# Forgetting attention with a spectral mix: one 8192 B row where two 4096 B rows of weights were loaded, with a spectrum shifted to fit

## The chip, the cores and the metric

The kernel runs on one core of one Trainium2 chip. The metric is the device time of one execution in microseconds (us). It is a single launch that reads all inputs from the chip's main memory (HBM) and writes the output there. A core has five engines that run side by side and meet through semaphores: TensorE (PE, the matmuls, with PEld for its weight loads), VectorE (DVE), ScalarE (ACT), GpSimd (POOL) and SyncE (SP). Transfers between HBM and the on-chip memory (SBUF, 128 partitions) run on 16 DMA engines; in this kernel POOL issues the loads and SP the stores. Matmuls write to PSUM, which DVE and ACT read.

## What is computed

Two steps, of which the second takes the first one's output.

```python
def _attn_ref(q, k, v, f):                      # [8, 8, 576, 64], f [8, 8, 576]
    scores = matmul(q, k.T) / sqrt(64)
    cum = cumsum(log(clip(f, 1e-4, 1.0)), axis=-1)
    scores = where(causal, -1e9, scores + cum[..., :, None] - cum[..., None, :])
    return matmul(softmax(scores), v)

def _moe_ref(x, w_r, w_i, w_ch):                # x [8, 576, 512], w_r, w_i [64, 512, 512]
    X = rfft(x, axis=1)                         # only the 64 lowest modes are mixed
    Xr, Xi = real(X[:, :64]), imag(X[:, :64])
    Yr = einsum('bmd,mde->bme', Xr, w_r) - einsum('bmd,mde->bme', Xi, w_i)
    Yi = einsum('bmd,mde->bme', Xr, w_i) + einsum('bmd,mde->bme', Xi, w_r)
    u = x + irfft(Y)                            # Y is 0 above mode 63
    return u + maximum(u @ w_ch, 0)
```

The inputs are f32. The weights w_r and w_i alone are 64 x 512 x 512 x 4 B x 2 = 134 MB, and each of their values is used once for the eight batches.

## The kernel before

**Stages.** First comes attention, in 32 pairs of heads (the loop over `i` with `scores`, `av`, `norm`, `trans`, `turn_v`, `back_v`); each pair's output goes to `x_all` as bf16, and `dft` (L546, L567) multiplies it with a basis of sines and cosines, which gives the 64 modes' spectrum. Then comes the *tail*, a loop over weight tiles that are left, and then the output: for 18 steps `base`, `rest` and the lines from L1013 to L1058 build `u` and `u @ w_ch` in PSUM, join them and store them.

**Units and chunks.** The 64 modes are taken as 16 units `u` of four modes. A unit's weights are four tiles (`u`, `dc`) of 1 MB in SBUF, `[128, 4096]` bf16, loaded from f32 with the type changed on the way. For `dc` 0 and 1 they hold rows 0 to 255 of the matrices. Tiles with `dc` 2 are w_r and with `dc` 3 w_i, rows 256 to 511, two neighbouring rows on each partition: a contiguous read of 2 x 512 x 4 = 4096 B per partition and mode, which lands as 2048 B. For `dc` below 2, units below 8 are read by single rows of 2048 B (L170) and the others as pairs of rows too (L179). `issue_w` issues the next tile of the list `wseq` on POOL; the code for `dc` 2 and 3 is L191.

**Where the tiles lie.** Most tiles come from `wpool`, seven buffers of 8 KB per partition, taken in turn; seven early tiles are `guests` in memory that is free then (`x_all`, `yx`). A load waits until PE has used the tile that had the buffer before. `wseq` begins with the 28 tiles of `early` (all of `dc` 0, and `dc` 1 of units 0 to 11), which are all multiplied between the attention's pairs, from the tenth on (`spec_early`). The tail then takes (u, 2), (u, 3) for units 0 to 11, and (u, 1), (u, 2), (u, 3) for units 12 and 13; then (15, 1), (15, 2), the three of unit 14, and (15, 3) last, in four parts of one mode. Three of the tiles are loaded in two cuts (`cuts`): 30 and 98 partitions, or 20 and 108.

**The spectrum.** For rows 256 to 511 it is `XP`, `[128, 2, 24, 64]`: partition p holds row 256 + 2p (index 0) and 257 + 2p (index 1), then 24 columns (minus imaginary, real, imaginary, for eight batches) and 64 modes. `by_pair` picks 16 columns of it that start at the real part for w_r and at minus the imaginary part for w_i. `spec_mms` (L229) multiplies a tile with it, eight matmuls of 512 columns for a tile (two rows x four modes), into the bank `A` of the unit. When the last tile of the unit is through, DVE adds what the early tiles gave (`Yb`, L906) and `to_rows` (L840 and the lines behind it) turns it into `YT`.

**What stands between the tiles.** In the tail's loop, `xw(b)` (L719 to L737, for eight units from 2 to 10) multiplies one batch of `x_all` with `w_ch` ahead of time, before the matmuls of the unit's `dc` 3. From unit 12 on, `folds` puts finished modes into `x_all` and `XW` (L743 to L796), with adds on POOL (L790). On L891 stand fillers: matmuls of 512 columns into a bank that nobody reads, four of them ahead of the fourth tile from the end of the list and eight ahead of the third; on L699 another eight ahead of the second. The very last tile is multiplied in `spec_cols` (L241), part by part.

**Order.** It is written by hand (`manual_schedule`): each engine takes its instructions in program order, and the framework adds the semaphore waits. `issue_w()` is called once behind each `spec_mms` of the tail.

Of the kernel before, what the change touches and what calls it, by code (L numbers as in the profile page):

```python
# [10 lines left out]
F32 = mybir.dt.float32  # L11
BF16 = mybir.dt.bfloat16
# [11 lines left out]
def kernel(  # L24
# [26 lines left out]
    NW = 7  # L51
    NX = 12
    NL = 8
    ML = 4 * NL
    XROW = 24 * ML + 32
    scale = 1.0 / math.sqrt(Dh)
# [5 lines left out]
    ctx.enter_context(tc.manual_schedule())  # L62

    const = ctx.enter_context(tc.tile_pool(name="const", bufs=1))
    wpool = ctx.enter_context(tc.tile_pool(name="wpool", bufs=NW))

    yx = const.tile([128, 8, 1280], F32, name="yx")
    x_all = const.tile([128, NEB, B, NSB, 128], BF16, name="x_all")
# [15 lines left out]
    wn = const.tile([128, NPAIR, 9], F32, name="wn")  # L84
    coef = const.tile([128, 1], F32, name="coef")
    accT = const.tile([128, NEB, B, 8], F32, name="accT")


    actx = ExitStack()
# [39 lines left out]
    early += [(u, 0) for u in range(NL, NU)] + [(u, 1) for u in range(NL, NX)]  # L129
    wseq = early[:]  # L130
    for u in range(NU - 2):
        wseq += ([] if (u, 1) in early else [(u, 1)]) + [(u, 2), (u, 3)]
    wseq += [(NU - 1, 1), (NU - 1, 2)] + [(NU - 2, dc) for dc in (1, 2, 3)] + [(NU - 1, 3)]
    wtile = {}
    wissued = [0]
# [8 lines left out]
        17: yx[:, 6:8, :].rearrange("p k e -> p (k e)").bitcast(BF16),  # L144
    }

    cuts = {(4, 2): (30,), (7, 2): (20,), (10, 2): (20,)}

    def by_rows(u, dc):

# [2 lines left out]
    def issue_w(half=None):  # L153
        n = wissued[0]
        if n >= len(wseq):
            return
        u, dc = wseq[n]
        if half != 1:
            if n in guests:
                t = 2 if by_rows(u, dc) else 4  # L160
                w8 = guests[n][:, 0 : 8 * D].rearrange("p (t m e) -> p t m e", t=t, e=D)
            else:
                shape = [128, 2, 4, D] if by_rows(u, dc) else [128, 4, 2, D]
                w8 = wpool.tile(shape, BF16, tag="w8", name="w8")
            wtile[(u, dc)] = w8
        w8 = wtile[(u, dc)]
        if by_rows(u, dc):
            for t, src in enumerate((moe_w_r, moe_w_i)):
                if half in (None, t):
                    nc.gpsimd.dma_start(  # L170
                        w8[:, t, :, :],
                        src[4 * u : 4 * u + 4, dc * 128 : (dc + 1) * 128, :].rearrange("m p e -> p m e"),
                    )
        elif dc < 2:
            src = (moe_w_r, moe_w_i)[dc]
            step = 4 if half is None else 2
            for j in range(2 * (half or 0), 4 if half != 0 else 2, step):
                m = 4 * u + j
                nc.gpsimd.dma_start(  # L179
                    w8[:, j : j + step, :, :].rearrange("p m r e -> p m (r e)"),  # L180
                    src[m : m + step, 0:256, :].rearrange("m (p r) e -> p m (r e)", r=2),
                )
        elif half != 1:
            src = (moe_w_r, moe_w_i)[dc - 2]
            ends = (0,) + cuts.get((u, dc), ()) + (128,)
            parts = [(0, 4, p0, p1) for p0, p1 in zip(ends, ends[1:])]
            if n + 1 == len(wseq):
                parts = [(j, 1, 0, 128) for j in range(4)]
            for j, step, p0, p1 in parts:
                m = 4 * u + j  # L190
                nc.gpsimd.dma_start(  # L191
                    w8[p0:p1, j : j + step, :, :].rearrange("p m r e -> p m (r e)"),
                    src[m : m + step, 256 + 2 * p0 : 256 + 2 * p1, :].rearrange(
                        "m (p r) e -> p m (r e)", r=2
                    ),
                )
        if half != 0:
            wissued[0] += 1
# [6 lines left out]

    XPv = XP[:].rearrange("p r c m -> p (r c) m")
    XQv = XQ[:].rearrange("p r c m -> p (r c) m")

    def by_pair(dc, c, n, m):

# [4 lines left out]

    def spec_mms(A, u, dc, first, last):
        w8 = wtile.pop((u, dc))
        for n in range(2):
            for j in range(4):
                m = 4 * u + j  # L220
# [445 lines left out]
    with ExitStack() as bctx:  # L666
# [13 lines left out]
            nc.vector.tensor_copy(BI4_il[grp, :, r % 2], BI4[grp, 512:576])  # L680
        perm_f = ypool.tile([128, 64], F32, name="perm_f")
        nc.vector.tensor_copy(perm_f[:], perm[:])
        XW = {}
        psT = bctx.enter_context(tc.tile_pool(name="psT", bufs=2, space=PSUM))
        psA = bctx.enter_context(tc.tile_pool(name="psA", bufs=2, space=PSUM))
# [1 line left out]

        def bank(where, name):
            return where.tile([128, D], F32, tag={id(psT): "t", id(psA): "a", id(psX): "x"}[id(where)], name=name)

        last64 = NSB - 1
        steps = [[(p, sb), (p, sb)] for p in (0, 1, 3, 2) for sb in range(last64)]
# [14 lines left out]
        with ExitStack() as mctx:  # L707
# [170 lines left out]
            for n, (u, dc) in enumerate(tail[:-1]):  # L878
                end = n + 1 == len(tail) or tail[n + 1][0] != u
                if n == 0 or tail[n - 1][0] != u:  # L880
                    first = dc
                    A = psA.tile([128, D], F32, tag="a", name="A1")
                if dc == NEB - 1 and u in xw_plan:
                    xw(xw_plan[u])
                if u >= NF:
                    folds(n + 2 == len(tail))
                    turn_rows()
                if n + 4 >= len(tail) > n + 2:
                    ps = bank(psT, "ps")
                    for _ in range(8 if n + 3 == len(tail) else 4):  # L890
                        nc.tensor.matmul(  # L891
                            ps[:], lhsT=ident_bf[:], rhs=wch[:, 0, :], start=True, stop=True
                        )
# [2 lines left out]
                    for k in range(8):  # L896
                        base_mm(U0[k % 2], 0, k % 2, 0, True)
                spec_mms(A, u, dc, dc == first, end)
                issue_w()
                if not end:  # L900
                    continue
                if u == NU - 1:
# [119 lines left out]
        for i in range(len(steps)):  # L1022
# [7 lines left out]
                rest(i + 1, 0, U)  # L1030
            rest(i, 1, Z)
            u_now = u_next
            o_sb = wpool.tile([128, 2, D], F32, tag="w8", name="o_sb")
            p, sb = steps[i][0]
            s0 = sb * 128
            if i in by_pool:
# [52 lines left out]
```

## Time and profile before

| what | us |
|---|---|
| three runs: lowest, median, highest | 434.15, 434.26, 434.43 |
| the profiled execution, its own time | 434.35 |
| its span, from the first instruction to the last | 432.6 |
| PE busy, share of the span | 344.1, 80% |
| DVE busy | 269.0, 62% |
| ACT busy | 220.0, 51% |
| POOL busy | 183.6, 42% |
| packets of the loads' DMA queue, as a share of 16 engines' span | 104.2% |
| packets of the stores' queue | 6.5% |
| DMA in the chain that ended last, share of the span | 36% |
| read from HBM, written to it | 163.73 MB, 9.44 MB |

Busy time on PE counts a matmul from its start to a modelled end, and overlapping ones once. The DMA queue's share can exceed 100% because two packets of one engine overlap in time. GB/s in the profile are counted by the bytes that land, which for weights, q and k is half of what is read. The granted clock (PEclk) is the share of full speed at which TensorE was allowed to run. The time of a load from issue to landing (30.9 us in the median for 1 MB tiles, 10 to 12 us for the loads in the attention stage) includes its wait in the queue behind earlier loads.

### The profile page before, as it was taken

How to read it: one execution, taken by the hardware profiler on the slowest of the kernel's cores; microseconds unless marked ns; L12 is line 12 of the kernel's file. 1: busy time of each engine (PE TensorE's matmuls, PEld its weight loads, DVE VectorE, ACT ScalarE, POOL GpSimd, SP SyncE). 2: the span in 40 equal slices, each digit the busy share in tenths (PEclk: the TensorE clock that was granted, in tenths of full speed). 3: DMA queues.
4: the chain of work that ended last, by engine and by line, in shares of the span. 5: the costliest groups of instructions: out<-in, count | busy, mean ns of one | idle time of the engine just before them, and what ended most of it. 6: DMA issues, size and time to landing. Idle time of an engine off the chain costs nothing.

```text
span 432.6 us, 10363 instructions
## 1 busy us (share of the span) xinstructions
PE 344.1 (80%) x4289; PEld 193.3 (45%) x4289; DVE 269.0 (62%) x660; ACT 220.0 (51%) x356; POOL 183.6 (42%) x272
## 2 busy tenths in 40 slices
PE   1698698989888888998989385487878498889993
PEld 0465466655565555556655142233334233333330
DVE  5788588876787889778786331222222266745794
ACT  4567467768677556767764022022232064441783
POOL 6554545445554544545312322112111089753284
PEclk9999799999999999999999789598998698989998
DMA  8999999999999999999999999999999999999498
GB/s 183 204 233 221 232 222 233 223 230 233 231 226 233 227 232 228 232 230 229 233 218 210 212 211 211 212 210 211 212 208 212 212 212 212 211 212 169 169 381 326
DMA packets 60783, 96.76 MB, mean 224 GB/s; under 512 B 4160, under 2 KB 29248, under 8 KB 60736
## 3 DMA queue, kind: packets, MB, share of 16 engines
q0 software_dynamic: 55040, 85.64, 104.2%
q1 hardware_dynamic: 5696, 10.47, 6.5%
q8 instruction: 33, 0.54, 0.5%
q14 instruction: 14, 0.11, 0.1%
HBM read 163.73 MB, written 9.44 MB: 400 GB/s over the span
## 4 chain that ended last, share of the span: by engine, by line
PE 38%; DMA 36%; DVE 15%; POOL 3%; ACT 3%; issue 3%; POOLq 0%; DVEq 0%; ACTq 0%
DMA w<-in_moe_w_i_dram 14%; DMA w<-in_moe_w_r_dram 13%; DVE qkT L388 6%; DMA x_all<-in_moe_w_i_dram 5%; PE A L229 5%; PE pd L567 5%; PE sps L461 5%; PE pd L546 4%; PE pav L514 4%; DVE vT L412 3%; DMA wch<-in_moe_w_ch_dram 3%; PE tv L410 3%; DVE x_all L530 2%; PE U L699 2%; PE Z L699 2%
## 5 line engine op out<-in xcount | busy, mean ns | idle before, releaser
L468 ACT ACTIVATE et<-sps 128x1024 bf16<-128x1024 f32 x96 | 93.1, 1025 | 11.8 <-PE sps L461 10.9
L514 PE MATMUL pav<-vs,et 128*128 128x65 bf16 (+1 forms) x896 | 50.9, 197 | 15.1 <-ACT e L455 14.7
L514 PEld LDWEIGHTS <-et 128*128 128x128 bf16 (+1 forms) x896 | 39.4, 102 | 34.6 <-issue 31.7
L388 DVE COPY qkT<-tp 128x640 bf16<-128x640 bf16 x64 | 48.8, 764 | 4.0 <-PE tp L383 4.0
L412 DVE COPY vT<-tv 128x576 bf16<-128x576 bf16 x32 | 24.2, 757 | 34.1 <-PE tv L410 33.3
L906 DVE TENSOR_TENSOR Yb<-A,yx 128x512 bf16<-128x512 f32 x15 | 10.3, 689 | 53.4 <-PE A L229 53.4
L229 PE MATMUL A<-w,XP 128*16 128x512 bf16 (+1 forms) x248 | 22.8, 448 | 24.8 <-DMA w<-in_moe_w_r_dram 15.7
L461 PE MATMUL sps<-qkT 64*128 64x512 bf16 (+4 forms) x320 | 39.5, 311 | 1.4 <-DVE qkT L388 1.3
L430 ACT COPY vs<-vp 128x640 bf16<-128x640 bf16 x32 | 22.3, 696 | 35.4 <-PE vp L422 35.4
L790 POOL TENSOR_TENSOR x_all<-um,x_all 128x512 bf16<-128x512 f32 x27 | 30.6, 1157 | 20.2 <-ACT um L789 20.0
L530 DVE TENSOR_TENSOR x_all<-pav,rcp 128x384 bf16<-128x384 f32 (+2 forms) x96 | 36.4, 379 | 3.3
L383 PE MATMUL tp<-ident_bf,qk 128*64 128x128 bf16 x576 | 29.8, 234 | 10.0 <-DMA qk<-in_k_dram 9.7
L730 PE MATMUL pxw<-wch,xT 128*128 128x512 bf16 x144 | 37.7, 420 | 0.0
L191 POOL DMA_DIRECT2D w<-in_moe_w_r_dram x19 | 14.0, 736 | 52.7 <-PE A L229 51.1
L737 ACT CAST yx<-pxw 128x512 bf16<-128x512 f32 x22 | 12.9, 585 | 35.3 <-PE pxw L730 35.3
L737 ACT CAST XW<-pxw 128x512 bf16<-128x512 f32 x14 | 8.2, 585 | 41.6 <-PE pxw L730 26.5
L112 POOL DMA_DIRECT2D qk<-in_k_dram x32 | 19.3, 604 | 16.8 <-DMA w<-in_moe_w_r_dram 4.7
L722 DVE COPY xT<-ptr 128x512 bf16<-128x512 bf16 (+1 forms) x32 | 13.7, 455 | 19.5 <-PE ptr L719 18.7
L112 POOL DMA_DIRECT2D qk<-in_q_dram x32 | 19.4, 607 | 14.4 <-DMA w<-in_moe_w_i_dram 7.0
L415 POOL COPY vT<-vT 128x64 bf16<-128x64 bf16 x32 | 7.8, 245 | 41.5 <-DVE vT L412 41.3
L383 PEld LDWEIGHTS <-qk 128*64 128x64 bf16 x576 | 19.4, 115 | 13.3 <-issue 9.3
L400 DVE TENSOR_TENSOR vn<-vt,wn 128x576 bf16<-128x576 f32 x32 | 23.9, 747 | 1.9 <-ACT wn L325 1.9
(159 smaller groups left out, 700.4 us busy)
## 6 DMA issues: line engine op xcount, KB each, us to landing
w<-in_moe_w_i_dram POOLq DMA_DIRECT2D x19, 1024.0 KB, 30.9
w<-in_moe_w_r_dram POOLq DMA_DIRECT2D x13, 1024.0 KB, 29.2
w<-in_moe_w_r_dram POOLq DMA_DIRECT2D x23, 512.0 KB, 11.0
w<-in_moe_w_i_dram POOLq DMA_DIRECT2D x19, 512.0 KB, 10.9
out_dram<-o_sb SPq DMA_DIRECT2D x36, 256.0 KB, 2.9
vt<-in_v_dram POOLq DMA_DIRECT2D x29, 288.0 KB, 10.8
qk<-in_q_dram POOLq DMA_DIRECT2D x32, 144.0 KB, 10.5
qk<-in_k_dram POOLq DMA_DIRECT2D x32, 144.0 KB, 10.0
```

The source lines that it names most:

```text
L112: nc.gpsimd.dma_start(qk[64 * n : 64 * n + 64, :, :], src[b, 2 * g : 2 * g + 2, :, :].rearrange("h (p r) d -> p h (r d)", p=64),)
L229: nc.tensor.matmul(A[32 * j : 32 * j + M, :], lhsT=lhsT, rhs=rhs, start=st_, stop=sp_)
L383: nc.tensor.transpose(tp[64 * hp : 64 * hp + 64, r - r0, :, :].rearrange("p n c -> p (n c)"), qk[:, hp, r * 64 : r * 64 + 64], ident_bf[:, :],
L388: nc.vector.tensor_copy(st[i]["T"][:].rearrange("p n (c r) -> p n c r", r=9)[:, :, :, r0:r1], tp[:, 0 : r1 - r0, :, :].rearrange("p r n c ...
L400: nc.vector.tensor_tensor(vn[:], st[i]["vt"][:], _strided(wn[:, widx(i), :], [[1, 9], [0, Dh]]), ALU.mult)
L412: nc.vector.tensor_copy(st[i]["vT"][:, 0:S].rearrange("p (c r) -> p c r", r=9), tv[:].rearrange("p r c -> p c r"))
L461: nc.tensor.matmul(ps[:, hp, c : c + n], lhsT=KT[sl, jb * 128 : jb * 128 + 128], rhs=QT[sl, i0 : i0 + n], start=True, stop=True,)
L468: nc.scalar.activation(st[i]["et"][:, T, :, :], ps[:], ACT.Exp, scale=scale)
L514: nc.tensor.matmul(pav[rows, sb % 3, hp, :], lhsT=eblk(i, hp, jb, sb), rhs=vs[:, 2 * jb + hp, :], start=(jb == 0), stop=(jb == sb),)
L530: nc.vector.tensor_tensor(x_all[rows, g, to, lo:hi, :].rearrange("p s (h d) -> p s h d", h=2), pav[rows, lo % 3 : lo % 3 + n, :, 0:Dh], _s ...
L730: nc.tensor.matmul(pxw[:], lhsT=xT[:, eb, sb * 128 : sb * 128 + 128], rhs=wch[:, eb, :], start=(eb == 0), stop=(eb == NEB - 1),)
L790: nc.gpsimd.tensor_tensor(xb, um.rearrange("p (g c) -> p g c", g=NEB), xb, ALU.add)
```

## The change

Tiles (u, 2) and (u, 3) of units 3 to 11 become one tile (u, 4) of 2 MB in two neighbouring slots. On its partitions 2k it holds four neighbouring rows of w_r (256 + 4k to 259 + 4k), on partitions 2k + 1 the same rows of w_i. So a read is 4 x 512 x 4 = 8192 B and lands as 4096 B, in two transfers of 64 partitions each. The matmuls are still 16 for a unit, now four rows x four modes, and each sums real and imaginary parts at once.

That needs a spectrum `XF[a]` (for row pair a of the four) whose even partitions hold the real columns and whose odd partitions hold the columns that start at minus the imaginary part, both for rows 4k + 2a and 4k + 2a + 1. In `XP`, pair a of the four rows stands on partition 2k + a. `shifts` makes two 128 x 128 matrices that move a value by one partition, and a mask of the even or odd partitions (`even`); `fours` computes, for each of eight pieces of 288 columns, the mask times the piece that already stands in place, plus the shifted other piece (a matmul). The results lie in the memory of `XS` and `Zt`. `shifts` stands ahead of tile (1, 2), `fours` ahead of (2, 2).

The pool `wpool` becomes a ring `wring` of seven slots with written-out places: pairs take slots 0-1, 2-3 and 4-5 in turn and slot 6 stays free for (12, 1). `held_slots` keeps account while the program is built, so that behind each `spec_mms` as many further tiles are issued as the free slots allow. The cuts move to (0, 2), (1, 2) and (2, 2). The four fillers ahead of the fourth tile from the end go, and the eight ahead of the third become four. The output's `o_sb` takes ring slots from slot 4 on.

```diff
+    QA, QB = 3, 12
-    wpool = ctx.enter_context(tc.tile_pool(name="wpool", bufs=NW))
+    wring = const.tile([128, NW, 8 * D], BF16, name="wring")
...
     for u in range(NU - 2):
-        wseq += ([] if (u, 1) in early else [(u, 1)]) + [(u, 2), (u, 3)]
+        wseq += ([] if (u, 1) in early else [(u, 1)])
+        wseq += [(u, 4)] if QA <= u < QB else [(u, 2), (u, 3)]
...
-    cuts = {(4, 2): (30,), (7, 2): (20,), (10, 2): (20,)}
+    cuts = {(0, 2): (30,), (1, 2): (20,), (2, 2): (20,)}
+    slot_of = {}
+    at = 0
+    for n, (u, dc) in enumerate(wseq):
+        if n in guests:
+            continue
+        if dc == 4:
+            at = 2 * ((u - QA) % 3)
+            slot_of[(u, dc)] = at
+            at = NW - 1
+        else:
+            slot_of[(u, dc)] = at
+            at = (at + 1) % NW
...
+        elif dc == 4:
+            for t, src in enumerate((moe_w_r, moe_w_i)):
+                nc.gpsimd.dma_start(
+                    w8[t:128:2, :, :, :].rearrange("p m r e -> p m (r e)"),
+                    src[4 * u : 4 * u + 4, 256:512, :].rearrange("m (p r) e -> p m (r e)", r=4),
+                )
...
+        if dc == 4:
+            for r in range(4):
+                for j in range(4):
+                    st_, sp_ = first and r == 0, last and r == 3
+                    M = 32 if st_ else 16
+                    nc.tensor.matmul(
+                        A[32 * j : 32 * j + M, :],
+                        lhsT=XFv[r // 2][:, 16 * (r % 2) : 16 * (r % 2) + M, 4 * (u - QA) + j],
+                        rhs=w8[:, j, r, :],
+                        start=st_,
+                        stop=sp_,
+                    )
+            return
...
+        def shifts():
+            nc.gpsimd.memset(shift[:], 0.0)
+            nc.gpsimd.tensor_copy(shift[:, 0, 1:128:2], ident_bf[:, 0:128:2])
+            nc.gpsimd.tensor_copy(shift[:, 1, 0:128:2], ident_bf[:, 1:128:2])
+            for o in range(2):
+                nc.vector.reduce_sum(even[:, o : o + 1], ident_bf[:, o:128:2], axis=mybir.AxisListType.X)
+
+        def fours():
+            for a in range(2):
+                for c in range(2):
+                    for h in range(2):
+                        own = XP[:, c, 8 - 8 * a + 8 * h : 16 - 8 * a + 8 * h, 4 * QA : 4 * QB]
+                        other = XP[:, c, 8 * a + 8 * h : 8 * a + 8 * h + 8, 4 * QA : 4 * QB]
+                        pf = bank(psX, "pf")[:, 0 : 8 * MF].rearrange("p (k m) -> p k m", k=8)
+                        nc.tensor.matmul(pf, lhsT=shift[:, a, :], rhs=other, start=True, stop=True)
+                        nc.vector.scalar_tensor_tensor(
+                            XF[a][:, 16 * c + 8 * h : 16 * c + 8 * h + 8, :],
+                            own, even[:, a : a + 1], pf, ALU.mult, ALU.add,
+                        )
...
-                if dc == NEB - 1 and u in xw_plan:
+                if (u, dc) == (1, 2):
+                    shifts()
+                if (u, dc) == (2, 2):
+                    fours()
+                if dc >= NEB - 1 and u in xw_plan:
                     xw(xw_plan[u])
...
-                if n + 4 >= len(tail) > n + 2:
+                if len(tail) == n + 3:
                     ps = bank(psT, "ps")
-                    for _ in range(8 if n + 3 == len(tail) else 4):
+                    for _ in range(4):
                         nc.tensor.matmul(
                             ps[:], lhsT=ident_bf[:], rhs=wch[:, 0, :], start=True, stop=True
                         )
...
                 spec_mms(A, u, dc, dc == first, end)
-                issue_w()
+                while wissued[0] < len(wseq) and not held_slots & slots(*wseq[wissued[0]]):
+                    issue_w()
...
-            o_sb = wpool.tile([128, 2, D], F32, tag="w8", name="o_sb")
+            o_sb = wring[:, (i + 4) % NW, 0 : 4 * D].bitcast(F32).rearrange("p (k e) -> p k e", k=2)
```

More of the change, by code (lines that the diff above doesn't have):

```diff
@@ L145, with slots @@
     }
-    cuts = {(4, 2): (30,), (7, 2): (20,), (10, 2): (20,)}
+    cuts = {(0, 2): (30,), (1, 2): (20,), (2, 2): (20,)}
[11 more added lines that the diff above has]
+            at = (at + 1) % NW
+    held_slots = set()
+    def slots(u, dc):
+        a = slot_of[(u, dc)]
+        return {a, a + 1} if dc == 4 else {a}
     def by_rows(u, dc):
@@ L161, in issue_w @@
                 w8 = guests[n][:, 0 : 8 * D].rearrange("p (t m e) -> p t m e", t=t, e=D)
-            else:
-                shape = [128, 2, 4, D] if by_rows(u, dc) else [128, 4, 2, D]
-                w8 = wpool.tile(shape, BF16, tag="w8", name="w8")
+            elif dc == 4:
+                a = slot_of[(u, dc)]
+                w8 = wring[:, a : a + 2, :].rearrange("p s x -> p (s x)").rearrange(
+                    "p (m r e) -> p m r e", m=4, e=D
+                )
+            else:
+                t = 2 if by_rows(u, dc) else 4
+                w8 = wring[:, slot_of[(u, dc)], :].rearrange("p (t m e) -> p t m e", t=t, e=D)
             wtile[(u, dc)] = w8
+            if n not in guests:
+                assert not held_slots & slots(u, dc), (u, dc)
+                held_slots.update(slots(u, dc))
         w8 = wtile[(u, dc)]
@@ L181, in issue_w @@
                     src[m : m + step, 0:256, :].rearrange("m (p r) e -> p m (r e)", r=2),
+                )
+        elif dc == 4:
+            for t, src in enumerate((moe_w_r, moe_w_i)):
+                nc.gpsimd.dma_start(
+                    w8[t:128:2, :, :, :].rearrange("p m r e -> p m (r e)"),
+                    src[4 * u : 4 * u + 4, 256:512, :].rearrange("m (p r) e -> p m (r e)", r=4),
                 )
@@ L207 @@
     XQv = XQ[:].rearrange("p r c m -> p (r c) m")
+    XFv = []
     def by_pair(dc, c, n, m):
@@ L217, in spec_mms @@
         w8 = wtile.pop((u, dc))
+        if wseq.index((u, dc)) not in guests:
+            held_slots.difference_update(slots(u, dc))
+        if dc == 4:
[11 more added lines that the diff above has]
+            return
         for n in range(2):
@@ L682 @@
         nc.vector.tensor_copy(perm_f[:], perm[:])
+        MF = 4 * (QB - QA)
+        XF = [
+            buf[:, 0 : 32 * MF].rearrange("p (k m) -> p k m", k=32)
+            for buf in (
+                XS[:].rearrange("p t x -> p (t x)"),
+                Zt[:].rearrange("p s m i -> p (s m i)").bitcast(BF16),
+            )
+        ]
+        XFv.extend(XF)
+        shift = ypool.tile([128, 2, 128], BF16, name="shift")
+        even = ypool.tile([128, 2], F32, name="even")
         XW = {}
@@ L689, in bank @@
             return where.tile([128, D], F32, tag={id(psT): "t", id(psA): "a", id(psX): "x"}[id(where)], name=name)
+        def shifts():
[14 more added lines that the diff above has]
+                            XF[a][:, 16 * c + 8 * h : 16 * c + 8 * h + 8, :],
+                            own,
+                            even[:, a : a + 1],
+                            pf,
+                            ALU.mult,
+                            ALU.add,
+                        )
         last64 = NSB - 1
```

## The prediction, on record before the changed kernel ran

> **What bounds the kernel now.** I read the page's slices first, then the windows by stage, then the end in order of time. All times are microseconds of the one profiled execution: 434.35 us, of which the span is 432.6 and 1.75 lies around it. The median of the three runs, 434.26, is 0.09 below it, so I work in the execution and take 0.09 off at the end. A difference under about 0.2% (0.9 us) I count as no change, because the three runs alone spread over 0.28.
>
> ```profile
> PE   1698698989888888998989385487878498889993
> PEclk9999799999999999999999789598998698989998
> DMA  8999999999999999999999999999999999999498
> GB/s 183 204 233 221 232 222 233 223 230 233 231 226 233 227 232 228 232 230 229 233 218 210 212 211 211 212 210 211 212 208 212 212 212 212 211 212 169 169 381 326
> ```
>
> Each digit is a fortieth of the span. DMA stands at 9 in every slice from the second to the 37th, while PE falls to 3 to 8 tenths in slices 23 to 32. GB/s counts bytes as they land. The weights are read as f32 and land as bf16, so 212 landed is 424 read. The kernel is a stream of 134 MB of weights and 29 MB of the rest, and until about 400 us the stream sets the time. The chain of waits does run through PE and DVE up to 240 us, but only because it steps from a load's issue back to what freed its buffer; the q and k loads there land 10 us after their issue for 0.7 us of transfer, so the queue is 10 us deep all along. The windows view (length, then busy time and count of PE, PEld, DVE, ACT and POOL, clock, DMA share, GB/s) shows where that ends:
>
> ```profile
> 60.00:120.00 60.00, 53.44 (x944) 35.38 (x938) 47.22 (x130) 43.28 (x71) 29.05 (x51) 1.00 1.21 230
> 280.00:300.00 20.00, 15.40 (x116) 7.41 (x115) 5.83 (x13) 5.27 (x9) 3.66 (x5) 0.92 1.12 211
> 380.00:390.00 10.00, 9.12 (x50) 4.16 (x50) 5.40 (x9) 4.15 (x8) 4.75 (x5) 0.83 1.12 212
> 390.00:402.00 12.00, 11.41 (x96) 5.02 (x95) 6.46 (x20) 1.30 (x4) 3.38 (x3) 1.00 0.75 140
> 402.00:415.00 13.00, 12.91 (x79) 4.16 (x78) 10.97 (x20) 11.09 (x22) 6.79 (x6) 1.00 0.69 259
> ```
>
> At 280 to 300 PE has a fifth of its time free and DMA none. From 380 on PE is full as well, and after 402 there are no loads left: PE, ACT and DVE make the output. The DMA share is above 1 because packets on one engine overlap. The hand-over is in the timeline (start, length, engine, line; in brackets PE's idle time before it):
>
> ```profile
> 375.39 0.66 PE L229 MATMUL A<-w,XQ 128*32 128x512 bf16 x8 [1.16 <-DMA w<-in_moe_w_i_dram]
> 380.34 0.65 PE L229 MATMUL A<-w,XP 128*16 128x512 bf16 x8 [1.28 <-DMA w<-in_moe_w_r_dram]
> ...
> 387.00 1.03 PE L891 MATMUL ps<-wch,ident_bf 128*128 128x512 bf16 x4
> 387.96 0.66 PE L229 MATMUL A<-w,XQ 128*32 128x512 bf16 x8
> ...
> 391.04 1.89 PE L891 MATMUL ps<-wch,ident_bf 128*128 128x512 bf16 x8
> 392.86 0.64 PE L229 MATMUL A<-w,XP 128*16 128x512 bf16 x8
> ...
> 396.26 0.65 PE L229 MATMUL A<-w,XP 128*16 128x512 bf16 x8
> 396.84 0.41 PE L241 MATMUL AT<-XP,w 128*128 128x16 bf16 x8
> ...
> 400.70 0.40 PE L241 MATMUL AT<-XP,w 128*128 128x16 bf16 x8
> ```
>
> The loads of units 15 (chunks 1 and 2) and 14 landed, by the trace's landing times, at 375.35, 380.30, 385.24, 390.22 and 395.15, and the four parts of the last one at 396.41, 397.66, 398.93 and 400.16. So PE still waits for DMA at 375 and 380, then falls behind: 2.7 late at 387.96, 2.6 at 392.86, 1.1 at 396.26, 0.5 at 400.70. Two fillers on L891, matmuls that nobody reads, stand in that stretch. The end is set by DMA to 0.5 us and by PE for the last bit.
>
> **Rows of 8192 B instead of 4096 B.** Units 3 to 11 read 9 x 2 transfers of 1 MB landed. Each transfer gives each of 16 DMA engines 32 rows (128 partitions x 4 modes / 16); after the change it is 16 rows of twice the length (64 x 4 / 16). So 18 x 16 = 288 rows fewer on each engine, with the same bytes. The trace has no packet of that length, so I bound it by three sizes that it has. Mean packet times in the loads' queue are 98.4 ns for rows landing 1024 B, 107.8 for 1152 and 173.4 for 2048: 0.0733 ns per byte. Landings of half-MB transfers follow each other at a median of 2.55 where they have 32 rows of 1024 (L170) and 2.48 where they have 16 rows of 2048 (L179): 0.07 / 16 = 4.4 ns per row spared. A 1 MB transfer takes 4.95 / 32 = 154.7 per row; less 2048 x 0.0733 = 150.1 that leaves 4.6 per row. Upper end 288 x 4.6 = 1.3 us saved; lower end from the v loads, whose four packets of 4608 B per engine land 0.72 apart, 0.0391 ns per byte read against 154.7 / 4096 = 0.0378: at that rate an 8192 B row costs 320 instead of 309.4, a loss of 288 x 10.6 = 3.1 us. I take 288 x 4.4 = 1.3, since all three weight rows lie on one line and v is another kind of transfer (f32 to f32, two 2304 B rows in a packet). That real and imaginary go to 64 partitions each costs nothing by the nearest row: q and k land on 64 partitions and still arrive 0.72 apart, 8 rows of 1152 at 90 ns, where the line gives 4.6 + 84.4 = 89.
>
> **Buffers and issue order.** Six of seven slots carry three pairs, the seventh idles until (12,1). Each pair is issued on POOL when PE has used the pair three units earlier; nothing waits between its two halves but an older load that PE has already used. When (u,4) has landed, two units are still queued, 19.8 us of transfer; PE's 16 matmuls (2 x 1.1) and an xw of some 7 us ahead of them leave over 10. First pair: slots 0 and 1 are free when (0,3) is used, about 238.5, while (2,3) lands only at 252.3. The DMA queue never runs dry: 0. On POOL no add stands before 347, so what is queued behind these waits is only further loads. At the end the last load is issued two tiles earlier in the program; it was already 20 ahead. The three cut transfers move to units 0 to 2 with their rows unchanged: 0. SP's order is unchanged, and its and DVE's new waits for old loads fall after 404, when all have landed at 400.2.
>
> **The new spectrum.** The nearest rows for the work:
>
> ```profile
> L1043 DVE SCALAR_TENSOR_TENSOR o_sb<-Z,u_sb 128x512 f32<-128x512 f32 x33 | 20.5, 683 | 2.6 <-PE Z L979 1.0 <-POOL o_sb L1048 0.7 <-DMA out_dram<-o_sb 0.5
> L849 DVE CAST YT<-yps 128x256 bf16<-128x256 f32 x12 | 5.1, 424 | 4.9 <-PE yps L840 4.9
> L415 POOL COPY vT<-vT 128x64 bf16<-128x64 bf16 x32 | 7.8, 245 | 41.5 <-DVE vT L412 41.3
> ```
>
> Eight DVE operations of 288 elements: 424 + 32 x 1.01 (the slope between the two DVE rows) = 457 ns, 3.7 us in all. Eight matmuls of 288 columns at about 0.3 (between 248 for 192 columns and 318 for 320): 2.4. On POOL a memset and two copies, about 1; on DVE two sums of 64, about 0.2 each. The matmuls fall where PE idles 2.69 before the load that lands at 247.33; four banks let PE through when the fourth DVE operation is done, about 246.9. The first reader is (3,4), landing near 262. POOL's share stands between the issues of (3,4) and (4,4), and the latter waits for PE until 243.5 anyway. All of it: 0. Without that cover, 4 us of PE late at 247 would still be swallowed by the queue of 10 us and more.
>
> **Fillers.** 12 become 4: minus 1.03 before 387.96 and minus 0.9 (half of 1.89) before 392.86. With nothing else changed PE would catch up with DMA and gain only its lateness, 0.5. With 1.3 off the stream: (15,2) at 380.3 - 1.3 = 379.0; (14,3) can start at 396.26 - 1.3 - 1.9 = 393.1, and lands at 395.15 - 1.3 = 393.9; the first part of the last load lands at 395.1, and from there PE needs the 3.86 that it needs now (396.84 to 400.70), so 399.0, against 398.9 for the landing of the last part. The last stage thus starts at 399.0 instead of 400.7.
>
> **Sum.** -1.3 (stream) - 0.4 (PE's lateness) = -1.7: 434.35 - 1.7 - 0.09 = 432.6 us.
>
> **Rivals.** (a) *The long rows bring nothing*, because each is cut in two: then only the lateness goes, 434.26 - 0.45 = 433.8. For it: no row of 8192 B is in the trace. Against it: packets of 4608 B are. The Trainium skill (DMA: Bandwidth & Descriptors, the part SWDGE vs HWDGE vs iDMA) says that a packet has preferably no more than 4096 B, which by bytes read would cut the new rows and give this rival's time; the 4608 B packets show that the limit is no hard one.
>
> (b) *PE cools at the end.* With the fillers gone, PE idles about 0.8 before (14,3) and 0.7 before the first part. After the waits of 1.28 and 0.40 at 379 to 382 the granted clock was 0.56 in 382 to 384 and 0.59 in 384 to 386. One such stretch of 3.4 us over the last 3.9 us of PE work costs 1.7 and gives 434.3; reaching into the output stage, up to 436. Against it: eight fillers on L699 remain, and the stretch 297 to 300 with 1.33 idle cooled while 314 to 317 with 1.43 did not. The Trainium skill (TensorE: Matmul & The Clock Gate, Part 1) has the clock fall only after an idle window of some 3.4 us; by that, nothing cools here and the forecast stands, but the 0.56 after a wait of 1.28 disagrees.
>
> (c) *Slower: long rows run at v's rate.* Price 3.1 on the stream, less the 0.5 that PE no longer adds: 434.26 + 2.6 = 436.9. It decides from 154.7 x 2 + 500 / 288 = 311.1 ns a row, beyond which nothing is gained, and from 314 the kernel is measurably slower. For it only the v packets; against it the line through three sizes.
>
> **How the numbers follow.** Forecast 0.58, (a) 0.13, (b) 0.14, half of it within 0.2% and half above, (c) 0.11, and 0.04 for something faster still. Faster is 0.58 + 0.04 = 0.62; same is 0.13 + 0.07 = 0.20; slower 0.07 + 0.11 = 0.18. The forecast's own range is 432.1 to 433.0 (3 to 6 ns spared per row, 0.9 to 1.7, and the 0.4). To hold 8 in 10 with (a) and most of (b), 431.6 to 435.6.
>
> **What would show it.** Right: GB/s of 214 to 215 landed in the slices of units 3 to 11 against 212; packets of 4096 B at about 324 ns each (173.4 + 150); pairs landing 9.76 apart against 9.90; last landing near 398.9; DMA at 9 throughout; PE's idle before (14,3) by DMA. Wrong: GB/s unchanged (a), PEclk below 1 after 390 (b), 209 or less (c), or a DMA slice below 9 around 240 to 260, which would mean that the buffers ran short.

## The result and the profile after

| what | before | after |
|---|---|---|
| median of six runs each, us | 434.20 (433.77 to 434.74) | 438.02 (437.15 to 440.12) |
| the profiled execution, its own time and its span | 434.35, 432.6 | 440.12, 438.3 |
| last landing of a weight | 400.16 | 401.86 |
| PE begins the last part of the last tile | 400.70 | 405.72 |

The change made the kernel slower: 1.0094 of the time before, 95% interval 1.0073 to 1.0114, that is 3.8 us by the medians. The forecast was 432.6, faster, with a range up to 435.6. The profiled execution is the longest of the six, so its stretches add up to 5.77 us and not to 3.8: 5.02 up to the last part of the last tile, 0.70 in the output stage, 0.05 outside the span.

Of the 5.02, 1.70 are loads that came in later as a whole: (14, 3) landed at 396.85 instead of 395.15. This lateness is older than the long rows, since (2, 3) already landed at 254.21 instead of 252.34. The held kernel (below) has the same instructions up to the issue of the last tile, and there (2, 3) landed at 250.42 and 250.79 in two traces. So the 1.70 belongs to this one execution; the 3.3 that are left are PE's lateness behind (14, 3), and they are what has to be explained.

The slices of the page of after, one digit or number for each fortieth of the span:

```profile
PE   1689798888888888998998683876863697489992
...
PEclk9999799999998999999999698699998599799998
DMA  8999999999999999999999999999999999993498
GB/s 178 205 234 220 232 220 233 231 225 231 232 230 226 234 225 235 225 235 225 236 210 193 210 215 215 212 215 214 215 215 212 212 213 211 212 211 70 172 381 312
```

GB/s reads 214 to 215 in most of slices 24 to 30, where the pairs land: the stream did become faster, as forecast. New are a 193 in slice 22 (below), and a PE that falls to 4 tenths in slice 35 (373 to 384), with 7 tenths of clock, where before it stood at 8. The windows of the same kernel (length, then busy time and count of PE, PEld, DVE, ACT and POOL, clock, DMA share, GB/s):

```profile
280.00:300.00 20.00, 16.29 (x121) 7.62 (x122) 5.53 (x12) 6.45 (x11) 2.45 (x4) 0.96 1.07 215
360.00:380.00 20.00, 11.53 (x74) 4.90 (x74) 10.21 (x18) 6.89 (x14) 12.95 (x15) 0.92 1.12 212
380.00:390.00 10.00, 8.12 (x45) 2.81 (x45) 5.87 (x11) 4.60 (x9) 6.02 (x6) 0.81 1.12 211
390.00:402.00 12.00, 11.02 (x74) 4.83 (x73) 7.56 (x14) 4.15 (x8) 6.76 (x6) 1.00 0.76 143
```

From 360 to 380 PE is busy for 11.5 of 20 us while the DMA share stays at 1.12: loads come in, and PE does not take them. What stopped it stands in POOL's timeline (start, length, engine, line, operation; in brackets the idle time before it and what ended it):

```profile
363.69 0.77 POOL L227 DMA_DIRECT2D wring<-in_moe_w_i_dram  x1
364.48 4.50 POOL L879 TENSOR_TENSOR x_all<-um,x_all 128x512 bf16<-128x512 f32 x4
368.93 1.12 POOL L227 DMA_DIRECT2D wring<-in_moe_w_i_dram  x2
372.57 0.53 POOL L227 DMA_DIRECT2D wring<-in_moe_w_i_dram  x1 [2.52 <-DMA wring<-in_moe_w_i_dram]
377.57 0.53 POOL L227 DMA_DIRECT2D wring<-in_moe_w_i_dram  x1 [4.48 <-DMA wring<-in_moe_w_i_dram]
378.12 3.37 POOL L879 TENSOR_TENSOR x_all<-um,x_all 128x512 bf16<-128x512 f32 x3
```

The four issues from 368.93 on are the four parts of (15, 3). Parts one and two go out at once, part three at 372.57 and part four at 377.57. Two loads landed just ahead of these: (13, 3) at 372.03 and (15, 1) at 377.04. Counted back in the order of the issues (parts three, two, one, then (14, 3), (14, 2), (14, 1), (15, 2), (15, 1)), (15, 1) is the eighth load before part four, and (13, 3) the eighth before part three. So an issue on POOL waited for the landing of the load that was issued eight before it. The trace's records say by what: the 192 loads report their landing on eight semaphores in strict turn (numbers 105 to 112), and ahead of parts three and four POOL carries out a wait for 111 and 112, the semaphores on which (13, 3) and (15, 1) report. The waits end at 372.07 and 377.08. The kernel's source has no such waits; the framework adds them. Before the change the parts went out behind (15, 1)'s matmuls, at 375.76 to 377.37, when both had landed (370.41 and 375.35), and nothing waited:

```profile
375.76 2.18 POOL L191 DMA_DIRECT2D w<-in_moe_w_i_dram  x4
```

Behind the waiting issues POOL's queue held the adds of `folds` (L879). The waits of the same kernel from 340 to 402 (engine, tile and line, what was waited for; total, times, longest) show who waited for those:

```profile
ACT um L878 <- POOL x_all L879: 11.4, 7, 7.8
...
POOL wring L227 <- DMA wring<-in_moe_w_i_dram: 7.0, 2, 4.5
...
PE pu L858 <- ACT y_sb L840: 6.1, 1, 6.1
```

and PE's timeline shows what came of it:

```profile
373.32 1.03 PE L843 MATMUL pyw<-wch,YT 128*96 128x512 bf16 x4
380.43 0.59 PE L858 MATMUL pu<-y_sb,BI 96*128 96x512 bf16 x1 [6.08 <-ACT y_sb L840]
...
401.29 0.64 PE L281 MATMUL A<-wring,XP 128*16 128x512 bf16 x8
...
405.72 0.40 PE L293 MATMUL AT<-XP,wring 128*128 128x16 bf16 x8
```

ACT could not write `um` anew until POOL had added the old one, ACT's next copy (`y_sb`) stood behind that, and PE stood still for 6.08 us. By the trace's clock records TensorE then had half its clock from 376.98 to 383.81. PE met (14, 3) at 401.29 although it had landed at 396.85: 4.4 late, against 1.1 before. The chain of waits (start, length, what) is the same story in order:

```profile
345.36 31.69 DMA wring<-in_moe_w_i_dram
...
377.57 0.53 POOL wring L227
378.12 1.17 POOL x_all L879
379.31 0.59 ACT um L878
379.90 0.49 ACT y_sb L840
...
380.43 0.59 PE pu L858
```

### The profile page after: what moved, and what is told of

Read it like the earlier page. It is cut to its first block, busy times and chain, and to the rows that moved or that the text cites. A ratio compares the mean times of both kernels' runs of the same rounds, so it can differ in the third digit from the quotient of the medians.

```text
span 438.3 us, 10338 instructions
## 1 busy us (share of the span) xinstructions
PE 339.6 (77%) x4277; PEld 191.9 (44%) x4289; DVE 272.7 (62%) x670; ACT 220.0 (50%) x356; POOL 181.7 (41%) x275
## 4 chain that ended last, share of the span: by engine, by line
DMA 45%; PE 27%; DVE 10%; POOL 7%; issue 6%; ACT 4%; POOLq 0%; DVEq 0%; ACTq 0%
DMA wring<-in_moe_w_i_dram 31%; DMA x_all<-in_moe_w_i_dram 5%; PE A L281 3%; DVE qkT L440 3%; PE sps L513 3%; PE pd L619 3%; DMA wch<-in_moe_w_ch_dram 3%; DMA vt<-in_v_dram 3%; DMA wring<-in_moe_w_r_dram 3%; PE pav L566 3%; PE pd L598 2%; DVE vT L464 2%; PE tv L462 2%; PE U L788 2%; DVE x_all L582 2%
## 5 line engine op out<-in xcount | busy, mean ns | idle before, releaser
L520 ACT ACTIVATE et<-sps 128x1024 bf16<-128x1024 f32 x96 | 93.0, 1024 | 13.9 <-PE sps L513 13.2
L879 POOL TENSOR_TENSOR x_all<-um,x_all 128x512 bf16<-128x512 f32 x27 | 30.5, 1155 | 10.8 <-ACT um L878 10.7
L819 PE MATMUL pxw<-wch,xT 128*128 128x512 bf16 x136 | 34.1, 395 | 1.0 <-DVE xT L811 0.6
L215 POOL DMA_DIRECT2D wring<-in_moe_w_r_dram x9 | 5.5, 615 | 66.7 <-PE A L262 40.7
L878 ACT COPY um<-pu 128x512 f32<-128x512 f32 x27 | 15.3, 587 | 19.4 <-POOL x_all L879 11.4
L598 PE MATMUL pd<-bas,x_all 128*64 128x96 bf16 (+3 forms) x240 | 22.0, 213 | 2.1 <-DVE qkT L440 1.1
```

Source lines behind the costliest of these rows:

```text
L520: nc.scalar.activation(st[i]["et"][:, T, :, :], ps[:], ACT.Exp, scale=scale)
L598: nc.tensor.matmul(pd[half, r, :, :] if r else pd[:, 0, :, :], lhsT=xs[:, r - 1 : 128 : 2] if r else xs, rhs=bas3[rows, sc, :, ML:NM] if r ...
L819: nc.tensor.matmul(pxw[:], lhsT=xT[:, eb, sb * 128 : sb * 128 + 128], rhs=wch[:, eb, :], start=(eb == 0), stop=(eb == NEB - 1),)
L879: nc.gpsimd.tensor_tensor(xb, um.rearrange("p (g c) -> p g c", g=NEB), xb, ALU.add)
```

## The experiments

Times are medians. The runs were made in three jobs; the kernel before, run in the same job, is 434.18 in the first (29 runs), 434.01 in the second (35) and 434.11 in the third (29). "Held" is the changed kernel with the last tile issued where the old kernel issued it.

**Hold the last tile's issue** (first job).

```diff
                 while wissued[0] < len(wseq) and not held_slots & slots(*wseq[wissued[0]]):
+                    if wissued[0] + 1 == len(wseq) and n + 6 < len(tail):
+                        break
                     issue_w()
```

> The changed kernel with one edit: the last tile (15, 3) is issued only behind the matmuls of (15, 1), as in the kernel before, and not two tiles earlier. Theory S (POOL stalls at the third and fourth part of the last tile until the loads issued eight earlier land at 372.0 and 377.0, and the adds behind them hold up ACT and PE): PE's idle stretch of 6.08 us at 374 to 380 goes, PE meets (14, 3) less than 1.5 us after it lands, and the time falls from 438.0 to 435 to 436, the rest being a last landing near 401.9 as now. Rival F (PE is late because the fillers are fewer and its clock fell in 377 to 384): the time stays at 437.5 to 438.5.

Measured: 433.09 (432.36 to 436.19, 12 runs), ratio 0.9983, interval 0.9964 to 1.0002. That is 4.9 below the changed kernel, for one tile issued later, and below the 435 to 436 expected, because the last landing did not stay near 401.9. POOL and PE of this kernel:

```profile
373.76 2.17 POOL L227 DMA_DIRECT2D wring<-in_moe_w_i_dram  x4
375.93 3.39 POOL L879 TENSOR_TENSOR x_all<-um,x_all 128x512 bf16<-128x512 f32 x3
```

```profile
374.18 0.66 PE L281 MATMUL A<-wring,XQ 128*32 128x512 bf16 x8 [1.53 <-DMA wring<-in_moe_w_i_dram]
...
393.99 0.64 PE L281 MATMUL A<-wring,XP 128*16 128x512 bf16 x8 [0.53 <-DMA wring<-in_moe_w_i_dram]
395.23 0.41 PE L293 MATMUL AT<-XP,wring 128*128 128x16 bf16 x8 [0.60 <-DMA wring<-in_moe_w_i_dram]
...
399.00 0.42 PE L293 MATMUL AT<-XP,wring 128*128 128x16 bf16 x8 [0.21 <-DMA wring<-in_moe_w_i_dram]
```

The four parts go out in 2.17 us without a gap, the adds follow at once, and PE's waits of over 0.5 us are for loads alone: 0.53 before (14, 3), 0.60 before the first part. The last landing was 398.96 and the last part began at 399.00; the forecast had 398.9 and 399.0 (how much of that is luck is said below).

**The early issue alone, in the old kernel** (first job).

```diff
                 issue_w()
+                if (u, dc) in ((13, 1), (13, 2)):
+                    issue_w()
                 if not end:
```

> The kernel before with one edit: one more tile is issued behind (13, 1) and behind (13, 2), so that the last tile goes out two tiles earlier. Theory S: POOL waits at parts three and four of the last tile for the landings of (13, 3) and (15, 1) at 370.4 and 375.4, PE gets an idle stretch of several us around 372 to 379, and the time rises by 1.5 to 4 us to 435.7 to 438. Rival F, and any theory in which POOL's order is harmless: 434.2 within 0.4.

Measured: 439.86 (438.87 to 440.68, 4 runs), ratio 1.0129, interval 1.0106 to 1.0152. Nothing of the long rows, the spectrum or the ring is in this kernel, and POOL stands as in after:

```profile
366.91 1.86 POOL L191 DMA_DIRECT2D w<-in_moe_w_i_dram  x3
370.40 0.53 POOL L191 DMA_DIRECT2D w<-in_moe_w_i_dram  x1 [1.63 <-DMA w<-in_moe_w_i_dram]
375.42 0.53 POOL L191 DMA_DIRECT2D w<-in_moe_w_i_dram  x1 [4.48 <-DMA w<-in_moe_w_i_dram]
375.96 3.38 POOL L790 TENSOR_TENSOR x_all<-um,x_all 128x512 bf16<-128x512 f32 x3
```

PE then idles 4.58 for `y_sb` (373.69 to 378.28), and its clock records show half the clock from 370.99 to 388.06. The early issue by itself costs 5.7 us, more than the 1.5 to 4 expected; how much of that is the stall and how much the clock that went with it, no run separates.

**Two parts instead of four, still early** (second job). If it is the eight loads in flight that count, two parts need two fewer of them.

```diff
-                parts = [(j, 1, 0, 128) for j in range(4)]
+                parts = [(j, 2, 0, 128) for j in (0, 2)]
```

> The changed kernel as it is, the last tile still issued early, but in two parts of two modes and not in four of one. Theory S in its exact form (a load waits for the landing of the load issued eight before it): the second part then waits for the eighth load before it, (13, 2), which lands near 367, so nothing stands still, PE's idle stretch at 374 to 380 is gone and the time is 433.3 to 434.5. If POOL's stall has another cause that comes with issuing that tile early (its buffer, the adds' order): 437 to 439 as in the changed kernel.

Measured: 434.6 (433.31 to 436.44, 10 runs), ratio 1.0018, interval 1.0000 to 1.0036.

```profile
367.62 1.45 POOL L227 DMA_DIRECT2D wring<-in_moe_w_i_dram  x2
369.28 2.28 POOL L879 TENSOR_TENSOR x_all<-um,x_all 128x512 bf16<-128x512 f32 x2 [0.22 <-ACT um L878]
```

Both parts go out before the old kernel's first, and no wait stands ahead of them: going out early is harmless, needing a ninth load in flight is not. Of the 2.47 by which its profiled execution is longer than the held one, 1.6 are a later stream (last landing 400.56 against 398.96; (2, 3) was already 2.35 later). The rest fits the coarser end: with two modes in the last part, the last mode begins 0.94 after the last landing, against 0.04 in the held kernel. That was not tried by itself.

**Early by one tile instead of two** (third job; held, with `n + 7 < len(tail)`).

> The last tile goes out one tile earlier than in the old kernel (behind (13, 3)) instead of two. Theory A (an issue waits for the landing of the load issued eight before it): the first three parts go out at once at about 371 to 374, since (13, 3) has landed by then, and the fourth alone waits for (15, 1), which lands at about 375 to 377: one wait of POOL of 2 to 4 us by DMA instead of 2.5 and 4.5, then PE idle 1 to 4 us for um, and 433.5 to 436, between the held kernel and the changed one. Rival (any early issue costs the whole amount, since it is the order of the adds and issues that matters and not the landing): 437 to 439.

Measured: 434.17 (433.05 to 435.26, 10 runs), ratio 1.0007, interval 0.9991 to 1.0023. POOL, then PE:

```profile
370.70 1.65 POOL L227 DMA_DIRECT2D wring<-in_moe_w_i_dram  x3
374.64 0.53 POOL L227 DMA_DIRECT2D wring<-in_moe_w_i_dram  x1 [2.29 <-DMA wring<-in_moe_w_i_dram]
375.19 5.59 POOL L879 TENSOR_TENSOR x_all<-um,x_all 128x512 bf16<-128x512 f32 x5
```

```profile
377.03 0.64 PE L858 MATMUL pu<-y_sb,BI 96*64 96x512 bf16 x2 [1.24 <-ACT um L878]
378.13 0.58 PE L858 MATMUL pz<-yw_sb,BI 96*128 96x512 bf16 x1 [0.47 <-ACT um L878]
```

Exactly the fourth part waits, for (15, 1), which landed at 374.12. Of the 2.29 on POOL 1.7 reach PE, 0.9 the last part (it begins 0.96 after its landing, against 0.04 in the held kernel), and 0.3 the median, which is within the noise. The rest fits PE's waits for loads that follow, which take up some of a delay; why two waits of together 7.0 cost so much more than one of 2.29 was not taken apart.

**The cuts moved early, in the old kernel** (first job): `cuts = {(0, 2): (30,), (1, 2): (20,), (2, 2): (20,)}`. The 193 in slice 22 made them a suspect: (1, 3) landed 6.36 after (1, 2).

> The kernel before with the cuts at (0, 2), (1, 2), (2, 2). Theory C (in the short queue at the end of the attention stage the engines that a cut spares run out of work, and the slowest engine is not relieved later): the last landing moves from 400.2 to 402 to 403.5, last minus median landing of the last tile from 1.45 to about 3, time 435.5 to 437. Rival B (the stream lost its time to the pairs of slots and the shallower buffers, not to the cuts): 434.2 within 0.4.

Measured: 434.8 (433.83 to 437.94, 12 runs), ratio 1.0011, interval 0.9992 to 1.0031. The last landing is 400.34, not 402 to 403.5, and the suspicion that the cuts cost 1.3 to 3 falls; from 235 to 260 this kernel moves 211 GB/s, the old one 212.

**Held, without cuts** (second job): `cuts = {}`.

> The changed kernel with the last tile held and no cuts at all. If the cuts do their work of relieving the slowest engines, last minus median landing of the last tile is above 2 us and the time 0.5 to 1.5 above the same kernel with early cuts (433.1): 433.6 to 434.6. If early cuts are worth nothing: 433.1 within 0.5.

Measured: 433.75 (433.17 to 434.8, 10 runs), ratio 0.9994, interval 0.9979 to 1.0009. It lies between the held kernel's two medians, 433.09 and 433.84 in the other jobs, so the time tells nothing. Last minus median landing is 2.12, above 2 as the first theory has it (held: 1.69 and 1.40), but two kernels with early cuts have 2.05 and 2.10 as well.

**The long rows taken apart again** (second job; held). Each pair is loaded in four transfers whose rows are 4096 B read, to the same places.

```diff
-                nc.gpsimd.dma_start(
-                    w8[t:128:2, :, :, :].rearrange("p m r e -> p m (r e)"),
-                    src[...].rearrange("m (p r) e -> p m (r e)", r=4),
-                )
+                rows = src[...].rearrange("m (p r) e -> p m r e", r=4)
+                for h in range(2):
+                    nc.gpsimd.dma_start(
+                        w8[t:128:2, :, 2 * h : 2 * h + 2, :].rearrange("p m r e -> p m (r e)"),
+                        rows[:, :, 2 * h : 2 * h + 2, :].rearrange("p m r e -> p m (r e)"),
+                    )
```

> The changed kernel with the last tile held, and each pair loaded in four transfers of 64 partitions with rows of 4096 B read, in place of two with rows of 8192 B: the same matmuls, slots and spectrum. If long rows spare 4.4 ns each: landed GB/s in the stage of units 3 to 11 falls from 214-215 to 211-212, and the time is 1.0 to 1.5 above that with long rows (433.1): 434.1 to 434.6. If the row length brings nothing: 433.1 within 0.4.

Measured: 435.14 (434.39 to 437.81, 12 runs), ratio 1.0028, interval 1.0012 to 1.0045; above the 434.1 to 434.6 expected, 2.05 above the held kernel of the first job, 1.4 above the one without cuts in its own job. Its window beside that of the held kernel (the first fence is this kernel, the second the held one):

```profile
280.00:300.00 20.00, 16.19 (x118) 7.89 (x119) 5.61 (x12) 6.03 (x11) 4.93 (x9) 0.91 1.12 211
```

```profile
280.00:300.00 20.00, 16.05 (x127) 7.98 (x129) 5.62 (x12) 6.18 (x11) 2.45 (x4) 0.91 1.07 215
```

Same bytes, same tiles: 211 against 215 GB/s. The number of issues changed too (9 against 4 on POOL in this window), and with four loads for a pair 32 issues between 215 and 340 us start 0.28 or 0.53 after the landing of the eighth load before them, where the held kernel has none. But the DMA share stays at 1.12, so the stream doesn't run dry, and the old kernel with early cuts has nearly the same pace with rows of 4096 B and no such waits (18 MB in 89.18 us against 89.49 here; table in the next section). So the pace is that of the rows.

**Held, with the old twelve fillers** (second job).

```diff
-                if len(tail) == n + 3:
+                if n + 4 >= len(tail) > n + 2:
...
-                    for _ in range(4):
+                    for _ in range(8 if n + 3 == len(tail) else 4):
```

> The changed kernel with the last tile held and with the twelve fillers of the kernel before. By the forecast's arithmetic PE then meets (14, 3) 1.1 us later less the idle 0.5 that it has there now, and the end comes 0.5 to 1.3 later: 433.6 to 434.4. If the fillers keep the clock up and pay for themselves: 433.1 or less.

Measured: 434.52 (432.91 to 436.0, 12 runs), ratio 1.0012, interval 0.9997 to 1.0027: 0.5 above the kernel before of its job, where the held one was 0.3 to 1.1 below in its own. Its profiled execution, at 433.68 shorter than the median, doesn't show that cost: the clock was 1.00 from 380 to 390, where before and held had 0.83, and the last part began 0.05 after it had landed.

**Held, with no fillers there at all** (third job; the block that begins with `if len(tail) == n + 3` removed).

> The held kernel without the four fillers that are left ahead of the third tile from the end. Theory (fillers there only delay PE, the clock stays at 1 without them): 432.3 to 433.2, at most 0.9 below the held kernel of the same job, and less where PE waits for the loads anyway. Rival (PE cools where the fillers go): a granted clock below 0.8 in 388 to 400 and 434 or more.

Measured: 433.64 (432.78 to 436.64, 10 runs), ratio 0.9999, interval 0.9977 to 1.002. Its window at the end:

```profile
390.00:402.00 12.00, 9.69 (x81) 4.00 (x81) 4.82 (x17) 2.10 (x5) 0.00 (x0) 1.00 0.62 116
```

PE idles 0.57, 1.46 and 0.61 before the last tiles and the clock is 1.00 through 390 to 402. The time lies above the 432.3 to 433.2 expected: nothing is gained over four fillers (0.2 against the held kernel of this job), and PE does not cool.

**Six pairs instead of nine, cuts moved with them** (first job; held, `QA` 6, cuts at units 3 to 5).

> The changed kernel with the last tile held as in the first run of this group, long rows for units 6 to 11 only, and the cuts at (3, 2), (4, 2), (5, 2), where more loads are queued. Theories S and C together, with 4.4 ns spared per long row: stream shorter by 12 x 16 x 4.4 ns = 0.85 us, last minus median landing 1.5 to 2, time 432.7 to 433.8. If the long rows bring nothing in the end: 434.0 to 434.5. If the pairs of slots cost time (rival B): above 434.5.

Measured: 433.73 (432.17 to 435.28, 12 runs), ratio 0.9989, interval 0.9972 to 1.0005. It lies between the held kernel and the one before, as two thirds of a small gain would, but neither end can be told from it.

**The held kernel again, in more rounds** (third job).

> The changed kernel with the last tile issued where the old kernel issues it, a second time and in more rounds. Theory A (the loss is the early issue alone; the rest of the change gives what was forecast): 432.5 to 433.5, about 1.1 below the kernel before, and an interval of the ratio that stays below 1. Rival (the change is worth nothing apart from the early issue): within 0.4 of the kernel before.

Measured: 433.84 (432.5 to 437.27, 12 runs), ratio 0.9992, interval 0.9965 to 1.0019. It misses what theory A expected: the gain is 0.3 here and was 1.1 in the first job. Over both, 24 runs have a median of 433.36. Without the early issue the change is worth 0.3 to 1.1 us, and neither interval excludes nothing.

## Why the prediction was wrong

**The step that failed** is in "Buffers and issue order": "At the end the last load is issued two tiles earlier in the program; it was already 20 ahead", priced 0. The loop that issues as much as there is room for moved the four parts of (15, 3) past two steps of the tail, and they stood on POOL ahead of the adds on L879. The prediction asked whether the data came in time and whether slots were free. It did not ask whether the issue itself could wait, nor what stands behind it on POOL in this stretch; the adds it did consider only at 347 and for the pairs. The runs put in its place: a load's issue waits for the landing of the eighth load before it; parts three and four waited 2.52 and 4.48; through the adds, `um` and `y_sb` PE lost 6.08. Taking this away gives 4.2 to 4.9 back; putting it alone into the old kernel costs 5.7; with fewer parts or one tile less it shrinks to what the count of eight says.

The count could have been made from the issue and landing times: where the four parts went, at 368.93, six loads ahead of them, (13, 3) to (14, 3), had still to land, and four more make ten. The limit of eight could have been read too. For the parts of (15, 3) no issue of the kernel before comes up against it, but in its attention stage 56 issues do: each starts 0.28 to 0.53 after the landing of the load eight before it, and POOL idles 71 us before them. Two of these, a q load behind a tile of weights and a k load behind a v load:

```profile
40.77 0.60 POOL L112 DMA_DIRECT2D qk<-in_q_dram  x1 [1.71 <-DMA w<-in_moe_w_i_dram]
...
171.14 0.59 POOL L112 DMA_DIRECT2D qk<-in_k_dram  x1 [0.40 <-DMA vt<-in_v_dram]
```

The prediction took such waits for waits for buffers alone ("what freed its buffer"). The rival on the slower side put its price on the rows; none put it on POOL.

**Long rows, -1.3: right as a mechanism, 1.0 to 1.4 in size, but little of it against the kernel before.** The 4608 new packets take 324.1 ns in the mean, against 324 in the forecast. In after the pairs' halves land 4.88 apart in the median and 4.90 in the mean, a pair 9.80 (forecast 9.76). The time from the landing of (2, 3) to that of (11, 3), which is 18 MB landed, by the landing times of the traces:

| kernel | rows read | cuts | (2, 3) lands | to (11, 3) |
|---|---|---|---|---|
| before, and the early issue in it | 4096 B | three in this stretch | 252.34, 251.86 | 88.34, 88.59 |
| before, cuts moved early | 4096 B | ahead of it | 251.66 | 89.18 |
| rows taken apart again | 4096 B | ahead of it | 254.67 | 89.49 |
| after | 8192 B | ahead of it | 254.21 | 88.16 |
| held, first and third job | 8192 B | ahead of it | 250.42, 250.79 | 89.04, 89.15 |
| five other kernels with the nine pairs | 8192 B | ahead of it, or none | 250.35 to 252.77 | 88.07 to 88.14 |

With no cuts in the stretch, long rows spare 1.0 to 1.4; in the two held traces one step of 5.84 or 5.89, where the others are 4.86 to 4.96, takes most of that back. Against the kernel before itself only 0.2 to 0.4 is left, since its three cuts had taken 0.6 to 0.8 off this stretch. So "the three cut transfers move to units 0 to 2 ...: 0" was wrong for this stretch. What the cuts gain ahead of it these traces can't tell: (2, 3) lands anywhere from 250.35 to 254.67.

The Trainium skill (DMA: Bandwidth & Descriptors, the part SWDGE vs HWDGE vs iDMA) has packets preferably at no more than 4096 B. The rows here travel as one packet each, 4096 B as landed, so the trace agrees if bytes are counted as they land, apart from the v loads' 4608 B. Rival (a), which this rule would have given by bytes read, did not come about. Rival (c) falls with the 4.90 between halves: 306 ns a row, against its 320.

**The end, -0.4: right as a mechanism, once nothing stands in front of it.** In the held kernel's profile the last part begins at 399.00, 1.70 before the old 400.70, with PE waiting for loads in front of it as forecast. That the time meets the forecast's 399.0 so closely is luck: in that execution (2, 3) had landed 1.92 earlier than before, ahead of the first long row, and the stretch of the long rows took 0.70 longer. By the medians the held kernel gains 0.3 to 1.1, not 1.7. Fillers: putting them back costs 0.8 to 1.6 by the medians (held kernels 0.3 to 1.1 below the kernel before of their jobs, this one 0.5 above), though the profile of that run doesn't show it. Rival (b), the cooling, falls with the 1.00 in 390 to 402.

**The output stage, forecast as unchanged: 0.4 to 1.2 too small.** From the start of the last part to the end of the span the three profiled kernels with the old code took 31.9 us each; those with the ring took 32.3 to 33.1. SP's timeline (start of the first store, time to the end of the last issue) for before, after and held, in three fences:

```profile
404.89 24.41 SPq L1058 DMA_DIRECT2D out_dram<-o_sb  x36
```

```profile
409.91 25.05 SPq L1152 DMA_DIRECT2D out_dram<-wring  x36
```

```profile
403.21 24.77 SPq L1154 DMA_DIRECT2D out_dram<-wring  x36
```

PE's share of the stage is the same, 24.3 to 24.4 from the last part to the last `Z`; the stores take longer. In before the last store goes out 0.68 after the one ahead of it, in the ring kernels 1.04 to 1.10. So the held kernel's profiled -1.27 is -1.70 for the loads and PE and +0.43 for the stage. What holds that last store wasn't tried, and stays open.

**New spectrum and 64-partition halves: 0, right.** PE's timeline of after has the spectrum's matmuls in a gap ahead of a load:

```profile
245.15 2.79 PE L770 MATMUL pf<-XP,shift 128*128 128x288 bf16 x8
...
249.64 1.10 PE L281 MATMUL A<-wring,XP 128*32 128x512 bf16 x8 [1.70 <-DMA wring<-in_moe_w_r_dram]
```

They take 2.79 (forecast 2.4), and after them PE still waits 1.70 for a load. The eight DVE operations take 0.50 each (forecast 0.457). The cuts moved early by themselves changed the old kernel's median by 0.6, within its interval.

**A sign that misled.** "A DMA slice below 9 around 240 to 260" was to mean that buffers ran short; DMA stayed at 9 while GB/s fell to 193 in slice 22. The dip was no sign of the change either. (1, 3) landed 6.36 after (1, 2) there, but 4.97 and 5.86 after it in the two traces of the held kernel, whose instructions are the same up to that point. So it varies from one execution to the next; what makes it vary wasn't settled.

## What to carry to other kernels

A load that is issued as soon as its buffer is free is not free: count the loads that are still to land, and look at what stands behind the issue on the issuing engine, because a wait there stops that engine's compute and everyone who waits for it. "As many as fit" is safe only with a limit on loads in flight beside the limit on memory. When a tile is split into parts, each part counts against that limit as a whole load. Such a limit shows in the trace beforehand, as issues that start just after the landing of an older load that has nothing to do with their buffer. And before a difference between two profiles is put down to a change, the stretch that the change can't touch has to be compared as well: here the executions differed there by 2 to 4 us.

## What the runs showed of the hardware that was not expected

- POOL issues no load until the load eight before it has landed: in all thirteen traces the loads take eight semaphores in turn, and no issue starts less than 0.28 us after the landing of the eighth load before it. The waits of 2.52, 4.48 (after), 1.63, 4.48 (the old kernel with the early issue) and 2.29 (early by one) each ended within 0.6 us of that landing. The limit that these traces show is that of the program's semaphore waits; whether the chip has one of its own, no run shows.
- Rows of 8192 B read, 4096 B landed, lie on the line of the shorter ones: 98.4 ns for 1024 B landed, 173.4 for 2048, 324.1 for 4096.
- One and the same kernel spreads by 5 us between executions (the kernel before 432.6 to 438.24 in the third job), more than the 0.28 of the first three runs let one expect. A gain of 1 us needs tens of runs, and 24 runs of the held kernel (median 433.36) against 93 of the kernel before (434.09, three jobs) are not too many for it.
